# Five buffers instead of four for the convolution's constants and inverse transforms, and a new instruction order, in a memory-attention and S4-convolution kernel

## The chip, the cores and the metric

The kernel runs on one core of one Trainium2 chip. The metric is the device time of one execution in microseconds; the kernel before is given as the median of its runs. The profile comes from one further execution, taken by the hardware profiler, whose own time is told apart below.

## The reference

Two branches work on the same input of 2048 tokens and 512 channels, and a gate per token mixes them. Branch a is attention with a compressive memory: 32 heads of 16 channels, 4 segments of 512 tokens, each segment attending to itself by softmax and to the earlier ones through a running state. Branch b is a state-space (S4) convolution, 2048 long, per channel; the reference does it by FFT.

```
def _A_ref(x, wq, wk, wv, wo, beta):
    ...                                          # q, k, v: (B, H=32, N=4, L=512, Dh=16)
    for s in range(N):
        logits = einsum('bhqd,bhkd->bhqk', qs, ks) * scale + mask
        p = softmax(logits);  a_dot = einsum('bhqk,bhkd->bhqd', p, vs)
        num = einsum('bhld,bhde->bhle', phi(qs), M)
        den = einsum('bhld,bhd->bhl', phi(qs), z)[..., None] + 1e-06
        outs.append(g * (num / den) + (1.0 - g) * a_dot)
        M = M + einsum('bhld,bhle->bhde', phi(ks), vs);  z = z + phi(ks).sum(l)
    return o @ wo
def _B_ref(u, A_re, A_im, B_re, B_im, C_re, C_im, log_dt, Dskip):
    P = exp(dt*A * l);  K = einsum('dn,dnl,dn->dl', Cc, P, dt*Bc).real
    y = irfft2(rfft2(pad(u)) * rfft2(pad(K)))[:L] + u * Dskip
    return y
x = A_x
g = sigmoid((x * gate_w).sum(-1, keepdims=True))
return g * _A_ref(x, ...) + (1 - g) * _B_ref(x, ...)
```

## The kernel before

The kernel is written as a graph. Python code (`build_graph`) makes 1799 operations, each with the tiles that it reads and writes: loads and copies by DMA, matrix products on PE (TensorE), evictions from PSUM on ScalarE (ACT) or VectorE (DVE), exponentials on ScalarE, products on VectorE. A long string, `ORDER`, then fixes the program: it lists the numbers of the operations in one global sequence, with a letter for the engine where an eviction may go to either (a is ScalarE, v or none VectorE) and with the number of the buffer that each new tile takes from its pool. `Sched.replay` walks the string and appends each operation to its engine's program; `Sched.emit` places the semaphore waits. Every engine works off its program in order. SyncE (SP) issues 254 DMAs, in the order of the string too, so a DMA whose data or buffer isn't ready holds up those behind it.

The work that the text speaks of, by the names used in it:

- The head (0 to about 40 us): parameters are loaded, powers of the state matrix are squared up step by step (ScalarE squares at line 857, casts at line 865; VectorE at lines 858, 859, 866, 869), copied across partitions by DMA, and multiplied into tables (VectorE, lines 1353 to 1365).
- The attention, by segment s and group of eight heads: scores on PE, exponentials on ScalarE (lines 1197 and 1244, 128x2048 each), products with v, normalization on VectorE (1158 to 1161), and a transposing DMA (line 1309) that turns the result for the final product.
- The lagged rows (lag0 to lag3): short matmuls that make the convolution's kernel for one quarter of the lags each; three evictions on ScalarE, then four DMA copies into the tile KTT. The Fourier matrices multiply KTT, so the first of them, K0, waits for the last copy of lag3.
- The convolution (`conv`), 32 tiles u of frequencies. For each: a load CD(u) of 128x896 constants (229,376 bytes: 640 columns for the kernel's transform, 256 for the inverse), the transform K(u) on PE, an addition on VectorE (1492), the product Y(u) with the transformed input (1496), the inverse transform V(u) on PE, its eviction, and a DMA that scatters it into the tile V2. The CD buffer comes free when V(u) is done on PE. The pools in question are CD (4 buffers of 1792 bytes a partition) and V (4 of 1024).
- The tail: the final products with the output weights, the last transforms of V2, the mix and the stores.

Evictions all go through one function, so they stand at line 229 (ScalarE) or 230 (VectorE), plain DMAs at line 225, and nearly all matmuls at line 711. The loop body around the change:

```
CD = Tile(CDP, BF16)
S.dma(lambda CD=CD: ap(CD, n=896), lambda u=u: hC[u], 229376, w=[CD], key=kx - 6)
V = Tile(VP, BF16)
...
op("PE", c_pe("F", 512, 512), fi, r=[CD, Y], w=[PI], acq=[V])
S.evac(lambda V=V: ap(V, n=512), lambda PI=PI: ap(PI, n=512), 512, r=[PI], pw=[V])
```

Of the kernel before, what the change touches and what calls it, by code (L numbers as in the profile page):

```python
# [382 lines left out]
15/0 216/0 17/0 9/5 16/0 39/7/0 40 10/1 0/0 33/2/0 34a 204/0 11/0 28/0 30/0 12/3 31/4 32a 42/3 49/0 43/10 50/5 67/0  # L383
41/1 44/9 45 48/2 46 24/0 200/0 201 18/2 27/0 35/0/1 14/2 13/3 1237/1 47 55/5 414/1 57/11 51/12 56/7 7/0 58/4 36a 25/0
19 202 52 203/0 53 60/5 59 72/1 68/6 70/1 71a/0 69v 54 61/0 62/13 20 21 187/7 74/2 23/0 37/4/2 207/7 73 84/2 211/3/3/2
75v/5 267/5/1/0 3/0 1/0 87v/9 63/6 1248/0/0 38a 86/3 85 76 77 1250/6 842/0 65/0 182/1 208/0 64 1245/1/1 98/5 96/2 97
212a 229/7/0/0 268a 185/1 88 107v/1 183/0 186/0 1243/4 1249a 223/3 104/3 1246a 190/2 1251a 99a/6 217/0 66 230 106/3
108 105 224a 272/5/1/1 213 209/0 1252 1253/1/0 184 1244v 80/4 218a 273 118/1 116/3 1255/3 214/4/0 215a 1037v/0 191
119v/3 221/6 274 78/1 117 231 222a 843/0 1254a 257/0/0 258 128/2 131v/0 219/1 1256a 275 188/0 130/3 89 1038v 210/0 129
109 79 259 1041v/0 140/3 312/3/0/1 220a 142/2 1039v 844 627/0 628/0 234/0/1 132 143a/2 235 236 1040v 232 1045 92/6 120  # L390
1042 22 141 270/1/1 152/2 400/0 239/0/2 240 269 271a 189 1043/0 154/0 133 1046 121 1247 1238/1/1 144 1257 313a 1258/0
1044 1050 233/2/0 276 226 227 241 153 243/0/3 1239a 244 145 164/1 155a/4 1047 167v/7 225 1240/3 401/1 1241a 228
358/3/2 629 1266/0/0 1051 1048/0 1052 277/0 156 237/2 238 168 245 251/0/1 169 1053 252 402 1049 242 246 166/2 247
1264/1 359a 90/0 417/3 165 1267a 253 254/0 1054 1057/0 1056 288/0/3 248/0 314 176a/8 249 1265a 289 177 1242 255 157
418a 315/1/0 256 250/0 1271/2/1 290 1055 178 284/0/1 316a 91 1268 1058 1279/1 100/3 1272a 260 285 1261/3/0 1062 1259/2
1059 1269/1 1060/0 286 102/0 1061 1270a 279/0/2 280 4/0 1273 1262a 281 1260a 1274/3/1 261 262/4 355/1/3/2 1276/2
302/0/0 303 356a 282/1 283 287 1263 1275a 6/0 1067/0 263 1063 317/3/0/1 264 1287/0/0 1277a 304 318 101 1064 1066 319
360/2/1/0 1278 361 1068 320 291 292 1069 363 296/0/2 1288a 297 1295/3/1 321/0 362 2/0 1297/2 364 1070/0 110/0 293/5
1065 1071 298 331/0/3 332 365 1296a 1300/0 294 112/5 111 1298a 1299 295/1 205 1072/3/0 1073 1074 1080/2 124/2 1076/0
1077 1081 1078 333 1075a 1089v/0 299/1 1090v 300 322/0/2 1079a 1088v 1029/1 1091v/0 206 1095 403 1282/3/1 122/3 123  # L400
1087a 1093/0 278 1092 1280/0 29/0 323 1283a 324 1096 357 1094 473/3/1 301 305 1100 306 307/5 81v/5 339/0/1 340 136/7
1098/0 1101 1082a 325/2 134/0 326 1281a 406/0/2/0 341 308 125v/6 1097 1102 309 474a 407a 408 1099 345/0/0 1284 346
342/3 1103 347 1308/0/1 366 137a/9 343 421/1 1309a 327/0/2 328 422a 329 113a/3 1107/0 265 1285/0 1286a 1289 135
427/1/0/1 1104 376/0/1 330 310 377 1106 428 429 378 114 1105 409/0/0 410a 334 335 1085/0 148/1 336/1 344 348 146/2
367/0/2 368 138 1301/1/0 369 349 337 1108 350/0 419/0 126 1112 338/0 420a 372/0/3 373 1302a 1110/0 370/0 1303/1 371
1109 103a/1 374 93a/0 139 470/2/1/1 1304a 1113 1111 384/0/2 385 115 430 1305 1116 351 94 147 471a 352 478/1/1/0 95
# [12 lines left out]
1176/4 1177 1178 1179a 500 465 1323/3/0 1324a 501 466 1343 516/0/4/0 517 528/1 559/0/2 560 561 530/0 518 529 519 576
467 567/1/2/1 1180/0 1181 1182a 1191a/0 568 534 1189v/0 1190a 1187a 569 1347/1 536/0/1 537 538 535/0 1188v 585 570  # L420
1334/0 1195 1193/0 1185 1196 1184 586 587 1183 1200 1192 556/2 557 468 1201 699/3/0/0 1348a 700 1414/3 545/0/0 546
644/0 701 547 5/0 1202 539/1 1194 540 1327/3 846 645a 1328a 541/0/3 542 742/0/1/2 543 743a 1203 638/1 266/0 311 1197
1325/4 745/3/0 1374/0 1204 594/0/1 595 1339/0/2 1370/1 746a 596 1340a 544 548 549 1198/0 606/0/0 607 1350/3/6 608 1356
1335/0 1329/2 1336a 1332 469/0 354 1186 558 562 1354 589/0/3 590 1205 550/4 744 591 551 1199 552/0 642/1 581/1 643a
609/0 610 1212 563 611 598/0/2 599 1398/1 1206 1355 564/3 1326/3/1 1402/4 1330 1207/0 1410/2 1213 1344 1395/1 592/1
1448/0 593 597 565 1208 1331 600 566 612/0/0 1214 613 614 633/3/0/1 634a 571 572 1399/2/5 635 601 1403 615 602 664/0/3
665 1404 1210/0 1386/1 1209 616 617/4 861/3/1 862a 857/2 1211 603/1 858a 1216 655/0/1 656 694/3/2 1411/2/0 1217/0 1333
604 618 695a 1218 619/0 650/0/1/1 651 605 1220/0 1219 863/1 864a 676/0/2 1215 1221 677 652 1415 1230/3/0 1231 1232a
520 1226/1 1227 1228 659/0/0 1229a 698/0 693 1416 399 1378/4 1030/0 660 588 653 1031/0 702 657 484 632/1 1345 1407/0
678 666 521 1222/3 1223 1224 1225a 639 580 1477/0 1365/2 1484/1 1491/2 661 856 859/2 860a 658/0 672/0/1 1233 1236 1235  # L430
# [110 lines left out]
def build_graph(nc, es, A_x, A_wq, A_wk, A_wv, A_wo, A_beta, B_A_re, B_A_im, B_B_re, B_B_im,  # L541
# [1126 lines left out]
```

## Time and profile before

| | us |
|---|---|
| runs of the kernel before: lowest, median, highest of 3 | 283.33, 283.72, 285.1 |
| the profiled execution: its time | 286.65 |
| the profiled execution: its span | 284.9 |
| mean granted TensorE clock in it | 0.993 |
| busy: PE, VectorE, ScalarE | 252.6, 261.2, 253.6 |

The span runs from the first to the last instruction that the profiler saw on the core; the time of the execution contains what lies around it, 1.8 us here. The page gives busy time by engine, the span in 40 slices, the chain of work that ended last (followed back from the end: at each step to what released it, or to the instruction before it on its engine), groups of instructions, and DMA issues. The views used besides are a table of the span by stages, the waits, and the time line of one engine in a window, where neighbouring instructions of one kind are put together with their count. In that view a number in brackets is the time that the engine stood idle before the row, with what released it. PEld is the loading of weights into PE, which overlaps its matmuls; SPq is SyncE's queue of DMA issues.

### The profile page before, as it was taken

What the parts mean: (1) busy time and instruction counts of PE and PEld (TensorE: products, weight loads), DVE (VectorE), ACT (ScalarE), POOL (GpSimd) and SP (SyncE); (2) the same over time, 40 slices, a digit from 0 to 9 for tenths busy, and PEclk for the clock granted to TensorE, in tenths of its full rate; (3) what the DMA queues carried; (4) which work ended last, traced back from release to release, by engine and by line L of the source; (5) the groups of instructions that cost most, each with busy time, mean ns of one, the idle gap of its engine ahead of it and who ended that gap; (6) DMA issues with size and microseconds to landing.
All of it is one profiled execution on the core that took longest, in us unless ns stands there. A gap on an engine that the chain in (4) does not pass through costs nothing.

```text
span 284.9 us, 9231 instructions
## 1 busy us (share of the span) xinstructions
PE 252.6 (89%) x3871; PEld 158.2 (56%) x3921; DVE 261.2 (92%) x616; ACT 253.6 (89%) x315; POOL 5.0 (2%) x10
## 2 busy tenths in 40 slices
PE   4969788788888889889999989799999999999996
PEld 1624454465556556575675657565565555555653
DVE  2997999999999999999999989989999999998474
ACT  5998999999999999899879999989999999987312
POOL 5000000000000000000000000000000000000000
PEclk9997999999999999999999999999999999999999
DMA  5999646422213354417665587877588877693217
GB/s 121 258 234 177 169 104 168 129 65 59 63 58 85 81 153 127 144 34 116 164 194 147 150 205 204 216 209 213 162 211 212 245 215 225 155 166 91 74 39 258
DMA packets 59756, 43.44 MB, mean 152 GB/s; under 512 B 36162, under 2 KB 53699, under 8 KB 59715
## 3 DMA queue, kind: packets, MB, share of 16 engines
q1 hardware_dynamic: 59714, 42.85, 57.9%
q8 instruction: 31, 0.51, 0.8%
q14 instruction: 11, 0.08, 0.1%
HBM read 21.04 MB, written 7.86 MB: 101 GB/s over the span
## 4 chain that ended last, share of the span: by engine, by line
PE 40%; DVE 24%; ACT 21%; DMA 7%; issue 5%; SPq 2%; ACTq 0%; DVEq 0%
PE psum L711 38%; ACT sb L1244 7%; DVE sb L1353 6%; ACT sb L229 6%; ACT sb L1197 5%; DVE sb L1362 5%; DVE sb L1356 4%; DMA sb<-sb 3%; DMA sb<-c_DN 2%; DVE sb L1365 2%; SPq L225 2%; DMA sb<-in_B_B_im_dram 1%; DVE sb L1161 1%; ACT sb L857 1%; ACT sb L1028 1%
## 5 line engine op out<-in xcount | busy, mean ns | idle before, releaser
L711 PE MATMUL psum<-sb 128*128 128x17 bf16 (+17 forms) x3783 | 246.7, 228 | 26.4 <-ACT sb L229 6.6
L711 PEld LDWEIGHTS psum<-sb 128*128 128x128 bf16 (+6 forms) x3833 | 152.0, 101 | 116.8 <-issue 21.1
L229 ACT ACTIVATE sb<-psum 128x512 bf16<-128x512 f32 (+4 forms) x144 | 84.5, 634 | 7.5 <-PE psum L711 5.2
L1244 ACT ACTIVATE sb<-psum 128x2048 bf16<-128x2048 f32 x40 | 75.6, 1890 | 3.5 <-PE psum L711 2.9
L1197 ACT ACTIVATE sb<-psum 128x2048 bf16<-128x2048 f32 (+1 forms) x40 | 70.1, 1752 | 2.8 <-PE psum L711 2.8
L1353 DVE TENSOR_TENSOR sb<-sb 128x4096 bf16<-128x4096 bf16 (+3 forms) x24 | 37.5, 1563 | 0.7 <-DMA sb<-sb 0.7
L1362 DVE TENSOR_TENSOR sb<-sb 128x512 bf16<-128x512 bf16 (+1 forms) x48 | 24.6, 528 | 0.0
L1256 DVE TENSOR_TENSOR sb<-sb 128x1024 bf16<-128x1024 bf16 (+1 forms) x40 | 22.7, 575 | 0.0
L1496 DVE TENSOR_TENSOR sb<-sb 128x1024 bf16<-128x1024 bf16 x32 | 21.6, 684 | 0.3
L1356 DVE TENSOR_TENSOR sb<-sb 128x2048 bf16<-128x2048 bf16 (+3 forms) x24 | 20.4, 850 | 0.0
L1492 DVE TENSOR_TENSOR sb<-psum,sb 128x256 bf16<-128x256 f32 (+1 forms) x32 | 17.6, 553 | 1.9 <-PE psum L711 1.7
L232 ACT ACTIVATE sb<-psum,sb 128x512 f32<-128x512 f32 (+2 forms) x10 | 6.5, 664 | 12.7 <-PE psum L711 12.7
L230 DVE CAST sb<-psum 128x512 bf16<-128x512 f32 x22 | 15.0, 684 | 2.2 <-PE psum L711 2.2
L1161 DVE TENSOR_TENSOR sb<-psum,sb 128x256 bf16<-128x256 f32 x32 | 13.1, 411 | 0.2
L1365 DVE TENSOR_TENSOR sb<-sb 128x512 bf16<-128x512 bf16 (+1 forms) x24 | 12.6, 527 | 0.0
L857 ACT ACTIVATE sb<-sb 128x512 f32<-128x512 f32 x18 | 12.0, 667 | 0.0
L1158 DVE RECIPROCAL sb<-psum 128x16 f32<-128x16 f32 x32 | 8.0, 250 | 2.6 <-PE psum L711 2.6
L858 DVE TENSOR_TENSOR sb<-sb 128x256 f32<-128x256 f32 x18 | 7.4, 416 | 1.4 <-ACT sb L857 1.3
L1298 DVE TENSOR_TENSOR sb<-psum,sb 128x512 bf16<-128x512 f32 x12 | 8.2, 685 | 0.2
L1028 ACT ACTIVATE sb<-psum 128x512 bf16<-128x512 bf16 x12 | 7.4, 631 | 0.7 <-PE psum L1025 0.7
L865 ACT ACTIVATE sb<-sb 128x512 bf16<-128x512 f32 x11 | 7.8, 709 | 0.0
L1079 ACT ACTIVATE sb<-sb 128x512 bf16<-128x512 bf16 x12 | 7.8, 646 | 0.0
(79 smaller groups left out, 127.4 us busy)
## 6 DMA issues: line engine op xcount, KB each, us to landing
sb<-sb SPq DMA_DIRECT2D x64, 128.0 KB, 3.3
sb<-c_DN SPq DMA_DIRECT2D x32, 224.0 KB, 3.4
scr_Z<-sb SPq DMA_DIRECT2D x16, 256.0 KB, 2.4
sb<-scr_Z SPq DMA_DIRECT2D x16, 256.0 KB, 3.4
sb<-in_A_x_dram SPq DMA_DIRECT2D x5, 512.0 KB, 4.6
sb<-c_DN SPq DMA_DIRECT2D x16, 160.0 KB, 3.3
out_dram<-sb SPq DMA_DIRECT2D x7, 256.0 KB, 2.2
scr_O<-sb SPq DMA_DIRECT2D x12, 128.0 KB, 3.2
```

The costliest lines, as they stand in the source:

```text
L229: fa = lambda e: e.activation(dst(), src(), ACT.Copy)
L711: mm = lambda e, o_, l, r_, st, sp, **kw: e.matmul(o_, lhsT=l, rhs=r_, start=st, stop=sp, skip_group_check=True, **kw)
L1161: op("DVE", ("V1", 256), lambda e: e.tensor_tensor(ap(o1, gi * 16, [[128, 4], [32, 4], [1, 16]]), ap(T, dims=[[68, 4], [17, 4], [1, 16]]), ...
L1197: o = op("ACT", ("Ax", 4 * n), lambda e: e.activation(ap(pT, dims=[[512, 4], [1, n]]), ap(P, dims=[[512, 4], [1, n]]), ACT.Exp, scale=0.25 ...
L1244: o = op("ACT", ("Ax", 2048), lambda e, P=P, pT=pT: e.activation(ap(pT, n=2048), ap(P, n=2048), ACT.Exp, scale=0.25), r=[P], w=[pT])
L1256: op("DVE", ("V2", 128 * nb), lambda e, pT=pT, dims=dims: e.tensor_tensor(ap(pT, dims=dims + [[1, 128]]), ap(pT, dims=dims + [[1, 128]]), ...
L1353: op("DVE", ("V2n1" if n == 1 else "V2", 512 * n), lambda e: e.tensor_tensor(ap(tile, 2 * dst, [[2 * (sp - dst), 2], [2 * ne, 128], [1, 2 ...
L1356: op("DVE", ("V2n1" if n == 1 else "V2", 256 * n), lambda e: e.tensor_tensor(D_(), D_(), ap(tile, 2 * sp + ne * 128, [[-ne * 128, 2], [2 * ...
L1362: op("DVE", ("V2x" if sstep > 2 else "V2", 256 * n), lambda e, half=half: e.tensor_tensor(run(t2, n, 0, 1) if half else run(tile, ne, dst, ...
L1365: op("DVE", ("V2", 256 * n), lambda e: e.tensor_tensor(D_(), D_(), ap(t2, n * 128, [[-n * 128, 2], [2 * n, 64], [1, 2 * n]]), ALU.add), r= ...
L1492: op("DVE", ("V1", 512 - 32 * c0), lambda e, K3=K3, PK=PK, c0=c0: e.tensor_tensor(ap(K3, 32 * c0, n=512 - 32 * c0), ap(PK, n=512 - 32 * c0 ...
L1496: op("DVE", ("V2", 1024), lambda e, Y=Y, XAB=XAB, K3=K3, Ke=Ke, xo=xo, u=u: e.tensor_tensor(ap(Y, dims=[[512, 2], [1, 512]]), ap(XAB, xo, ...
```

## The change

Two pools get a fifth buffer each: CD, for the transform constants, and V, for the evicted inverse transforms. The V pool thereby overlaps in memory with one more pool of the earlier stage, whose last readers are the lagged matmuls. The rest is a wholly new `ORDER`: the same 1799 operations in another sequence, with other buffer numbers. The counts of instructions on each engine stay as they are; of the evictions that may go to either engine, ten move to VectorE and ten to ScalarE. A line of the string is shown for its form.

```diff
 ORDER = """
-15/0 216/0 17/0 9/5 16/0 39/7/0 40 10/1 0/0 33/2/0 34a 204/0 11/0 28/0 30/0 12/3 31/4 32a 42/3 49/0 43/10 50/5 67/0
...
+16/0 9/0 15/0 216/0 30/0 17/0 39/3/0 10/3 0/0 33/6/1 40 34a 414/1 31/0 204/0 28/0 11/2 32a 49/3 12/1 42/7 67/1 41/0
...
     V2aP = mkpool("V2a", 16384, 1, 2)
-    CDP = mkpool("CD", 1792, 4, 2)
+    CDP = mkpool("CD", 1792, 5, 2)
     XsPs.append(mkpool("Xsb", 4096, 3, 2))
     K3P = mkpool("K3", 1024, 4, 2)
     YP = mkpool("Y", 2048, 4, 2)
-    VP = mkpool("V", 1024, 4, 2)
+    VP = mkpool("V", 1024, 5, 2)
```

**SyncE at the start of the convolution**, before. The rows of shape 128x1x160 are the four copies of lag3; 128x896 are loads of CD (the two in a row behind 128x640, a load of another constant, are CD1 and CD2; the one behind the copies is CD3); the transposing DMA belongs to the attention.

```order
L225 DMA sb<-c_DN 128x896
L225 DMA sb<-c_DN 128x640
L225 DMA sb<-c_DN 128x896 x2
L225 DMA sb<-sb 128x1x160 x4
L225 DMA sb<-c_DN 128x896
L225 DMA sb<-scr_Z 128x1024
L225 DMA sb<-sb 64x1024
L225 DMA scr_O<-sb 128x4x128
L225 DMA sb<-c_DN 128x640
L1309 DMA_TRANSPOSE sb<-scr_O 128x1x512
```

The same place now: CD1, two copies, CD0 and CD3, the third copy, the transpose, the fourth copy.

```order
L225 DMA sb<-c_DN 128x896
L225 DMA sb<-sb 128x1x160 x2
L225 DMA sb<-c_DN 128x896 x2
L225 DMA sb<-sb 128x1x160
L1309 DMA_TRANSPOSE sb<-scr_O 128x1x512
L225 DMA sb<-sb 128x1x160
L225 DMA sb<-scr_Z 128x1024
L225 DMA sb<-c_DN 128x896 x2
```

The four copies stood together; now two loads of CD stand between the second and the third, and the transpose between the third and the last.

**ScalarE at the same place**, before. 128x40x12 and 128x40x8 are the three evictions of lag3, 128x2048 are exponentials.

```order
L1244 ACTIVATE sb<-psum 128x2048
L229 ACTIVATE sb<-psum 128x40x8
L229 ACTIVATE sb<-psum 128x40x12
L1244 ACTIVATE sb<-psum 128x2048
L229 ACTIVATE sb<-psum 128x40x12
L229 ACTIVATE sb<-psum 128x32x16
L1244 ACTIVATE sb<-psum 128x2048
```

And now:

```order
L1244 ACTIVATE sb<-psum 128x2048
L229 ACTIVATE sb<-psum 128x40x12 x2
L229 ACTIVATE sb<-psum 128x40x8
L1244 ACTIVATE sb<-psum 128x2048
L229 ACTIVATE sb<-psum 128x32x16
L1244 ACTIVATE sb<-psum 128x2048
```

The third eviction moved ahead of the exponential.

A little later on SyncE, CD10, CD7 and CD6 stand in this order (before: CD7, CD10, then the load Zx4 of transformed input, then CD6; now: CD10, CD7, the store of V0, CD6, and Zx4 seven places behind CD6). With five buffers CD6 takes the one that V3's matmuls free; before, it took the one that V4's freed. On PE, K6 stands at the same place of its program, with V5 now directly ahead of it instead of X15 (one matmul).

In the head, the parameter C_re goes to another buffer and is loaded ahead of C_im; of the powers, one square on ScalarE moves ahead of two evictions, and the cast of the seventh power behind an exponential, a square, an eviction and another cast.

**PE at the end of the program**, before. The run of 30 wide matmuls (128x512) holds five of K31, the last score block of four, and 21 behind it; 128x17 are products of exponentials with v.

```order
L711 MATMUL psum<-sb 128x512 x30
L711 MATMUL psum<-sb 128x17 x8
L711 MATMUL psum<-sb 128x512 x2
L711 MATMUL psum<-sb 128x17 x32
L711 MATMUL psum<-sb 128x512 x7
L711 MATMUL psum<-sb 128x128 x8
L711 MATMUL psum<-sb 128x512 x59
L711 MATMUL psum<-sb 128x256 x12
```

And now, where the first two rows are the last score block:

```order
L711 MATMUL psum<-sb 128x384 x4
L711 MATMUL psum<-sb 128x128 x4
L711 MATMUL psum<-sb 128x512 x3
L711 MATMUL psum<-sb 128x17 x24
L711 MATMUL psum<-sb 128x512 x12
L711 MATMUL psum<-sb 128x17 x16
L711 MATMUL psum<-sb 128x512 x6
L711 MATMUL psum<-sb 128x128 x8
L711 MATMUL psum<-sb 128x512 x57
L711 MATMUL psum<-sb 128x256 x12
```

Behind the last score block stood 21 + 2 + 7 + 59 = 89 wide matmuls, and now stand 3 + 12 + 6 + 57 = 78. The load of the output weights moved back in SyncE's program, to its 244th place of 254.

More of the change, by code (lines that the diff above doesn't have):

```diff
@@ L468 @@
[L468 to L470 removed]
+16/0 9/0 15/0 216/0 30/0 17/0 39/3/0 10/3 0/0 33/6/1 40 34a 414/1 31/0 204/0 28/0 11/2 32a 49/3 12/1 42/7 67/1 41/0
+44/1 13/4 14/5 24/0 48/4 45 27/0 50/2 18/1 19 20 200/0 201 46 1237/0 43/13 55/0 51/8 47 57/10 56/5 52 202 7/0 53 25/0
@@ new lines @@
+58/6 203/0 54 35/6/2 36a 60/2 68/2 59 72/1 69v/0 74/1 70/5 71a 73 84/2 182/0 21 62/0 1/0 187/3 37/7/1 38a 85/4 87v/9
+3/0 207/3 86 211/4/0/2 63/3 75v/6 267/0/1/0 88 99a/0 23/0 96/2 1243/6/0 268a 188/3 208/0 76 1248/3/1 1250/2 98/5 97
+842/0 272/5/0/1 185/1 89 212a 104/0 1251a 1245/7 61/9 190/2 107v/1 1244v 229/0/1/0 64/0 209/0 230 1249a 66 213 191/0
+77 106/7 1246a 189 108 105 210/0 116/2 186 183/3 1252 273 1255/2/1 109 117/6 118 217/4 1247 221/6 218a 222a 128/0
+119v/3 274 1253/3 65 130/1 184 275 223/7 214/4/0 224a 215a 78/3 231 120 131v/5 1256a 257/0/0 258 80/7 79 259 22
@@ new lines @@
+289 359a 254/1 255 290 1055 256 260 100/0 315/2/0 418a 316a 4/0 1268 248/1 1057/0 284/0/2 249 285 286 1056 250/0 1058
+1062 1269/3 1270a 1261/0/0 178 1060/0 404/0 1059 1273 279/0/1 280 1259/2 1063 1274/3/1 261 1262a 281 1260a 355/0/3/2
+262/4 1061 263 356a 101 1067/0 1066 314 1276/2 264 302/0/0 303 1064 282/0 283 287 1263 1287/1/0 1275a 1277a 317/3/1/1
+360/2/0/0 291 292 1278 304 296/0/1 297 1068 318 320 1288a 319 1070/0 293/3 361 362 294 1069 1297/1/1 363 1295/3 298
+321/2 364 1071 331/0/3 1296a 299/3 332 1298a 1299 1065 1080/1/0 6/0 300 8/0 295/1 1076/0 1077 1081 205 365 110/2
@@ new lines @@
+335 419/3 1109 350/2 1301/2 420a 1111 125v/3 82 83 430 336/5 1116 1117/0 1112 372/0/1 1302a 373 370/3 337 371 1083
+405/1 95 470/2/1/1 351 2/0 103a/4 374 138 384/0/3 146/3 385 1084 471a 386 1118 352/1 148/4 375 379 139 1305 1306/1
+1307a 478/2/1/1 479 380 338 114 390/0/2 391 415/0 392 147 1119 387/1 388 389 126 1113 408 1120/0 353 480 1313/2/0 1085
+432/0/0 433 1114 1121 393 394 416a 646/0/0 423 481 1115 366 1314a 434 395/5 381/3 441/0/1 396 442 425 149v/9 1310
+1122/2/0 1123 115 647a 382 1126/0 1124 158/0 1127 397/1 1128 383 443 5/0 159/7 431/1/1 1125a 192/5 160 170/2 1130/3
@@ new lines @@
+1157/0 1154 692a 1158 1155 162 163 494/0/1 495 1341/0 1160/0 446/1 526/1/0 531/0/1/1 460/2 447 1159 461 448/1 488/3
+496 489 493 502/0/0 1161 503 412 497 1166 1167/0 462 1338/2/1 1168 532 527a 1162 533 1342 265 504 508/0/2 509 475/1
+505/1 574/0/0/1 498 510 506 575a 553/0/0 554 1163 555 1169 1164 1170/0 1165 1349/3 1321/0 507 636/0/1 1370/2 511 512
+1346/2 637a 513/3 1351/5/1 1352a 1334/0 1398/1 1171 499/5 463/3/0/0 528/0 464 582/4/0/0 583 1322/1 514 845 1172/0/0
+1176/5 1173 1174 1175a 1177 1178 500 465 1179a 530/0 476 501/0 515 1323/3/0 516/0/2/1 584 579/1 466 517 1343 1324a
@@ new lines @@
+1206 563 564/2 610 1208 611 591 598/0/2 599 643a 1326/0/5 1213 565 1330 592/2 593 1331 597 600 566 1214 1402/4 571
+612/0/3 613 633/0/2/1 1344 614 1356 1399/3/0 634a 635 1403 601 1404 639 1209 615 616 664/0/0 1332 1374/3 311 602
+861/0/1 1210/0 665 617/3 862a 572 857/3 858a 469/0 655/0/2 656 694/0/2 695a 1414/1 1211 603/0 1216 618 1217/0 619/1
+650/3/1/0 1218 651 1386/4 1407/0 1184 744 1220/0 863/1 864a 676/0/1 1411/0/2 1415 677 1219 1215 1221 1226/1/0 652 1345
+520 1222/3 1223 1224 1225a 604 1416 693 1227 1228 1229a 1365/1 653 521 1230/0 580 1231 484 1232a 659/0/3 1484/3 660
@@ new lines @@
+1490/0 1419/0 1500 1494/3 1362/3/3 1390/0 1368 1501/0 752 1513/1/1 716 1369 1495/0/3 1496a 712 713 714 723/0/1 1514
+729 1506/1/0 1515/3 1388/0/2 1366 717 718 1507 724 1547/0 1367 1502/1/1 1526/3 1389a 735/3/4/1 1384/4 1483 1503a
+1519/1 1385a 1497 856 1408/5/0 1508/2 1509/3/2 1409a 736 725 737 719/0 738 720 802 722/0 726 730 1510a 1511 1394
+806/0/1 721/1 705 731 796/1 732/3 1032 684/1/1/0 797 1393 1387/1/7 807 1391 733 810/0/3 685 753 847/1 734 1527/0/3 686
+1392 1548/1/0 747/0 1561/4 687 1516/2/0 739 740 1520/3/2 808 1371/2 1528 811 1423/4/2 1517a 1424a 1412/5 1413a 1549
@@ new lines @@
+962 967/1 959 1003/0/0 1669/1 1661 963 1657a 970 971 964/5 965 966/0 975 976 977/4 978 979 941/0 1687/2 1473/3/2 1474v
+1004 841 942a 1471/2 1472a 994/0/3 984/1 985a 1469 1658 1670/0/3 1671a 1023/1/0/1 1651 1707/1 1708 1005 1476 1662/2
+1727/0 1728 1729a/0 1024 1025 1026 1709v/0 1688/2/3 1676/3 1689 1733/0 1695/3/0 995 996 998/0/2 1475 1696 1697/0
+1677/2/0 997/1 1734 1637 1678v 1735v/1 1701/3 1680/1 1702 1698/2/2 1679 999 1000 626 1699a 1690/1 1011/0/1 1012
+1681/0/0 1682 1663/2/4 1001 1002 1672 1006 1013 1007/0 1683/3 1008 1009/1 1015/0/3 1740/0 1703v/1 1664a 1010/2 1014
@@ L471 @@
+1783 1785v 1786a 1787
 """
```

137 lines of the change are left out of this document (50 added, 87 removed).

## The prediction

> **What bounds the kernel now.** I read the busy line of the page first, then the span cut into stages, then the chain that ended last, and at the places it names the time line of each engine.
>
> ```profile
> PE 252.6 (89%) x3871; PEld 158.2 (56%) x3921; DVE 261.2 (92%) x616; ACT 253.6 (89%) x315; POOL 5.0 (2%) x10
> ```
>
> Three engines are within four per cent of one another, so the page's shares name no bound. The stages do; the columns are the length and the busy time of PE, PEld, DVE, ACT and POOL, then clock, DMA share and GB/s.
>
> ```profile
> 0.00:27.00 27.00, 19.75 (x136) 10.39 (x139) 19.75 (x61) 22.04 (x42) 3.73 (x8) 0.94 0.95 207
> 27.00:120.00 93.00, 78.87 (x1563) 50.72 (x1578) 92.05 (x211) 91.90 (x122) 0.65 (x1) 1.00 0.40 108
> 120.00:165.00 45.00, 41.84 (x867) 29.38 (x878) 44.79 (x109) 41.88 (x51) 0.67 (x1) 1.00 0.53 130
> 165.00:190.00 25.00, 22.20 (x293) 15.21 (x293) 22.86 (x60) 22.68 (x25) 0.00 (x0) 1.00 0.81 213
> 190.00:262.00 72.00, 70.08 (x888) 40.07 (x899) 68.51 (x160) 68.96 (x69) 0.00 (x0) 1.00 0.73 194
> 262.00:282.60 20.60, 19.89 (x137) 12.45 (x138) 13.23 (x22) 6.15 (x10) 0.00 (x0) 1.00 0.31 109
> ```
>
> The head waits for transfers. From 27 to 165 VectorE is idle for 0.95 + 0.21 = 1.2 us of 138, so nothing but work taken off it helps there. From 165 to 282.6 PE is busy for 112.2 of 117.6 us: 2.80 + 1.92 + 0.71 = **5.4 us** of idle time are all that an order can win there. The largest pieces of it stand in the chain of the convolution's start (start, length, what):
>
> ```profile
> 161.67 3.98 DMA sb<-sb
> ...
> 165.74 1.74 PE psum L711 x18
> ...
> 178.02 0.62 PE psum L711 x3
> 178.64 6.35 DMA sb<-c_DN
> ...
> 185.04 5.21 PE psum L711 x53
> ```
>
> Two transfers end waits: the last copy of the lagged kernel rows, for which K0 waits at 165.74, and the constants of K6 (CD6), issued at 178.64 when V4's matmuls have released a buffer. The time lines give what the engines lost there (in brackets the idle time before, and its releaser).
>
> ```profile
> 165.74 1.74 PE L711 MATMUL psum<-sb 128*128 128x256 bf16 x18 [0.52 <-DMA sb<-sb]
> ...
> 185.04 5.21 PE L711 MATMUL psum<-sb 128*128 128x256 bf16 x53 [1.36 <-DMA sb<-c_DN]
> 186.45 1.57 ACT L229 ACTIVATE sb<-psum 128x512 bf16<-128x512 f32 x3 [1.57 <-PE psum L711]
> 185.80 0.42 DVE L1492 TENSOR_TENSOR sb<-psum,sb 128x256 bf16<-128x256 f32 x1 [0.27 <-PE psum L711]
> 188.52 0.69 DVE L230 CAST sb<-psum 128x512 bf16<-128x512 f32 x1 [1.10 <-PE psum L711]
> ```
>
> At K6 all three stop for about the same time: PE 1.36, ScalarE 1.57, VectorE 0.27 + 1.10 = 1.37. That is a stall with nothing beside it, and worth its length.
>
> **The buffers and K6.** A load of c_DN usually takes half of what CD6 took (least, median, most):
>
> ```profile
> DMA to landing us min/median/max: 2.3/3.4/6.4
> ```
>
> SyncE's issues around it:
>
> ```profile
> 175.12 2.62 SPq L225 DMA_DIRECT2D sb<-c_DN  x2
> 178.21 0.32 SPq L225 DMA_DIRECT2D sb<-scr_Z  x1
> 178.64 0.36 SPq L225 DMA_DIRECT2D sb<-c_DN  x1
> ```
>
> The two ahead are CD7 and CD10; CD10, freed by V3, is the second of the first row, whose bar ends at 175.12 + 2.62 = 177.74. With five buffers CD6 takes what V3 frees, one convolution tile earlier, and Zx4, a transfer of 256 KB, comes behind it. An issue takes 0.32 us, so CD6 goes out at about 177.74 - 0.32 = 177.42, 1.22 us earlier, and at the same 6.35 us lands at 183.77. PE came free for K6 at 185.04 - 1.36 = 183.68. What is left of the wait is 0.09, and V5's two matmuls now stand ahead of K6. **I take -1.3 us**; bounds 0 (it lands no earlier, because it is the queue that is slow) and -1.57, ScalarE's gap. On average the 32 loads get about 3 us more between release and use, but this is the only load that this trace shows PE waiting for:
>
> ```profile
> PE psum L711 <- DMA sb<-c_DN: 1.4, 1, 1.4
> ```
>
> So the other 31 loads' lead is priced at nothing, and so is the fifth buffer of the V tiles: no eviction of an inverse transform waited for its slot here.
>
> [...]
>
> **The lagged rows and K0.**
>
> ```profile
> 157.20 1.99 ACT L1244 ACTIVATE sb<-psum 128x2048 bf16<-128x2048 f32 x1
> 158.96 1.19 ACT L229 ACTIVATE sb<-psum 128x480 bf16<-128x480 f32 x2
> 159.78 3.63 SPq L225 DMA_DIRECT2D sb<-sb  x4
> 163.45 0.59 SPq L225 DMA_DIRECT2D sb<-c_DN  x1
> ...
> 166.42 1.29 SPq L1309 DMA_TRANSPOSE sb<-scr_O  x1
> ```
>
> Before, two of the three evictions of the lagged rows stand ahead of the 1.99-us exponential on ScalarE and the third behind it, and the four copies go out back to back from 159.78. After, all three evictions stand ahead of the exponential, but between the copies stand two loads of CD and a DMA transpose: 0.32 + 0.59 + 1.29 = 2.2 us of issuing, by the last two of these rows and, for CD0, the 0.32 us that an issue took at 178.21. How much earlier can the third eviction be? PE's run with its matmuls, and the loads that wait for the same matmuls:
>
> ```profile
> 156.68 1.27 PE L711 MATMUL psum<-sb 16*128 16x384 bf16 x56 [0.29 <-ACT sb L1244]
> 157.98 1.75 SPq L225 DMA_DIRECT2D sb<-c_DN  x4
> ```
>
> The run ends at 156.68 + 1.27 = 157.95, so the eviction can come forward from 158.96 by 1.0 us. If a copy lands as long after its issue as now, K0 comes 2.2 - 1.0 = 1.2 us later. Two smaller things work the other way: one of the four loads that went out ahead of the copies comes behind them (1.75/4 = 0.4), and PE has one short block less ahead of the lagged matmuls (0.2, an estimate from the length of such a block in its order). **I take 1.2 - 0.6 = +0.6**; bounds -0.5 (PE's wait of 0.52 goes) and +2.2 (nothing comes earlier). Behind K0 in PE's order stand K1, score blocks and the whole convolution, so a delay there is passed on; VectorE is idle for only 2.1 us from 165 to 190 and ScalarE for 2.3, and half of that already belongs to K6.
>
> **The head.** The load of C_re loses a wait on SyncE's queue, since it no longer reuses a buffer that PE reads. Two waits of VectorE are touched by the new order:
>
> ```profile
> SPq L225 <- PE psum L796: 2.0, 1, 2.0
> 26.83 0.76 DVE L858 TENSOR_TENSOR sb<-sb 128x256 f32<-128x256 f32 x2 [1.35 <-ACT sb L857]
> 39.46 2.29 DVE L1353 TENSOR_TENSOR sb<-sb 128x4096 bf16<-128x4096 bf16 x1 [0.67 <-DMA sb<-sb]
> 33.57 5.80 DMA sb<-sb
> ```
>
> The 1.35 us for a square on ScalarE should go, because that square stands earlier there. The 0.67 us for a copy of a power (the last row, issued at 33.57) should grow: its cast on ScalarE stands behind an exponential now and three smaller operations,
>
> ```profile
> 30.43 1.91 ACT L1197 ACTIVATE sb<-psum 128x2048 bf16<-128x2048 f32 x1
> 32.19 0.67 ACT L857 ACTIVATE sb<-sb 128x512 f32<-128x512 f32 x1
> 35.56 0.71 ACT L865 ACTIVATE sb<-sb 128x512 bf16<-128x512 f32 x1
> ```
>
> which moves its end by some 3.3 us to 33.9 and its issue from 33.57 to 34.2 at the earliest: 0.6 late. VectorE and ScalarE share the work of the next stage, so what one of them alone wins or loses counts half: -1.35/2 + 0.6/2 = **-0.4**; bounds -1.35 and +0.7 (the second wait doubles and the first stays).
>
> **The tail.** After the last score block 78 wide matmuls and 12 of half width are left, instead of 89 and 12. Their price is the pitch near the end, where 49 wide and 12 half ones ran:
>
> ```profile
> 270.00:281.80 11.80, 11.75 (x61) 1.00 0.33 122
> ```
>
> 11.75/(49 + 6) = 0.214 us, so 11 x 0.214 = 2.4 us of PE work move ahead of the last exponentials. PE is busy there too (70.08 of 72 us from 190 on), so moving work out of the tail shortens nothing unless it fills idle time. The load of the output weights is issued later, near 244 of 254, with about 1 to 2 us to spare. **I take 0**; bounds -1.9 (all of PE's idle time of 190 to 262 is filled) and +0.5 (a weight late by that much).
>
> Ten evictions go to VectorE and ten to ScalarE:
>
> ```profile
> L229 ACT ACTIVATE sb<-psum 128x512 bf16<-128x512 f32 (+4 forms) x144 | 84.5, 634 | 7.5 <-PE psum L711 5.2
> L230 DVE CAST sb<-psum 128x512 bf16<-128x512 f32 x22 | 15.0, 684 | 2.2 <-PE psum L711 2.2
> ```
>
> At 634 and 684 ns a pair costs neither engine more than 0.05 us each way, and the counts of instructions stay: nothing, with bounds of 0.5 either way.
>
> **Sum.** -1.3 + 0.6 - 0.4 + 0 = -1.1 us. The profiled execution took 286.65 us, 1.8 more than its span of 284.9, and its sum is 285.55. The median of the runs is 283.72, or 0.9898 of the profiled one, and 285.55 x 0.9898 = **282.6 us**.
>
> **Rivals.** (a) The waits only change places and the time stays, 283.7. For it: from 165 on three engines are near their limit, and a released stall of 1.3 meets the +0.6 and whatever comes late next, such as Zx4, now behind CD6. Against it: at K6 all three engines stood still. (b) The longer lead also removes the short waits of PE that the chain doesn't name: half of 5.4 us, and 0.7 of the head, 3.4 together: 283.25 on the profiled scale, **280.4**. Against it: most of these waits are for ScalarE and not for loads. (c) Slower: the last lagged copy goes out behind the DMA transpose, K0 is 2.2 us late, every slot of the convolution is released so much later, and CD6's gain is lost with them: 286.65 + 2.2 = 288.85, **285.9**. It decides whether the third eviction leaves ScalarE more than about 1.6 us earlier than 159.7; if not, this holds. (d) The fifth buffer is there but the loads go out as before, since SyncE issues in order and is held by something else ahead of them; only +0.6 - 0.4 remain: 286.85, **283.9**.
>
> **How the numbers follow.** Forecast 0.46 (own range 281.3 to 283.6), (a) 0.18, (b) 0.18, (c) 0.12, (d) 0.06. The bounds of the terms add up to -5.8 and +3.9; not all fall on one side. The range reaches to (b) and nearly to (c): 280.0 to 285.6. A difference under about 1% (2.8 us) is what a measurement of this kernel can't tell from none. Faster by more means under 280.9: most of (b) and an edge of the forecast, 0.20. Slower by more means over 286.6: an edge of (c), and something late that I don't see, 0.09. Within 1%: 0.71.
>
> **What would show it.** In the profile after: CD6 issued near 177.4, relative to K0, and PE's wait for c_DN gone (first term); PE's idle time before K0 at about 1.1 us, still ended by a copy (second); VectorE's 1.35-us wait gone and that at L1353 at 1 us or more (third); from the last score block to the end the span shorter by about 2.4 us, with PE's idle time from 190 on unchanged near 2.6 (fourth). A new wait for a DMA of over 2 us anywhere behind 165 would make the prediction wrong upwards; PE's idle time behind 165 under 3 us, downwards.

## The result, and the profile after

The kernel with the change took 283.25 us (median of 20 runs, 282.55 to 284.47). The kernel before, run beside it, took 285.51 us (20 runs, 282.78 to 291.21). The ratio is 0.9946 with a 95% interval of 0.9923 to 0.9968: half a per cent faster, within the range of the forecast and under the one per cent that the prediction called no change. (The ratio leaves out executions that lie over 1.5% above the fastest of their kernel, so it is nearer to one than the two medians.) The lowest times of the two kernels, 282.78 and 282.55, are almost the same. What differs is the spread, and that turned out to be the subject of this case.

The page of the profiled execution (283.67 us, span 281.9), busy line and granted clock:

```profile
PE 256.6 (91%) x3921; PEld 156.5 (56%) x3921; DVE 260.0 (92%) x616; ACT 254.5 (90%) x315; POOL 5.0 (2%) x10
PEclk9999999999999999999999999999999999999999
```

And the clock row of the page of before:

```profile
PEclk9997999999999999999999999999999999999999
```

The fourth slice of before, 21 to 28 us, has a 7: for a part of it PE's granted clock was lower. The prediction read the row of stages with its 0.94 for the head and passed over it. The same stages after the change:

```profile
0.00:27.00 27.00, 18.65 (x146) 9.24 (x150) 21.64 (x70) 23.60 (x43) 3.69 (x8) 1.00 0.83 192
27.00:120.00 93.00, 82.00 (x1651) 51.76 (x1653) 92.14 (x211) 92.19 (x125) 0.65 (x1) 1.00 0.46 122
120.00:165.00 45.00, 42.47 (x821) 28.21 (x816) 43.79 (x103) 41.43 (x46) 0.66 (x1) 1.00 0.49 122
165.00:190.00 25.00, 24.68 (x322) 16.40 (x320) 24.79 (x64) 23.92 (x27) 0.00 (x0) 1.00 0.77 217
190.00:262.00 72.00, 71.82 (x897) 40.54 (x896) 68.18 (x157) 66.52 (x66) 0.00 (x0) 1.00 0.72 188
```

From 165 to 262 PE is busy for 96.50 of 97 us. The first place where the two executions part is the head. PE's time line there, before and then with the change:

```profile
18.48 0.38 PE L711 MATMUL psum<-sb 128*128 128x512 bf16 x1
21.35 4.18 PE L711 MATMUL psum<-sb 128*128 128x512 bf16 x25 [2.49 <-ACT sb L229]
```

```profile
17.25 2.12 PE L711 MATMUL psum<-sb 128*128 128x512 bf16 x9
20.04 0.39 PE L711 MATMUL psum<-sb 128*128 128x512 bf16 x1 [0.68 <-ACT sb L229]
20.62 1.04 PE L711 MATMUL psum<-sb 128*128 128x512 bf16 x4 [0.19 <-ACT sb L229]
22.11 1.04 PE L711 MATMUL psum<-sb 128*128 128x512 bf16 x4 [0.46 <-ACT sb L229]
```

Before, PE has a pause of 2.49 us; with the change it is cut up into 0.68, 0.19 and 0.46. The windows of before that follow the pause (length, PE's busy time, granted clock, DMA share, GB/s) show what comes of it:

```profile
21.00:22.00 1.00, 0.65 (x2) 0.74 1.17 339
22.00:23.00 1.00, 1.00 (x4) 0.50 1.00 136
23.00:24.00 1.00, 1.00 (x4) 0.50 1.09 234
24.00:25.00 1.00, 1.00 (x4) 0.55 1.10 249
25.00:26.00 1.00, 0.69 (x24) 1.00 1.29 116
```

PE works at a granted clock of 0.50 from 21.49 to 24.90, 3.41 us, and so does 1.7 us less, an estimate (half of 3.41). The clock's next change in this profile is at 284.32, behind PE's last matmul: 259.42 us later, which is 76 times 3.413. The exponentials of this execution start 1.5 us later than the same ones with the change around 45 us, and 1.9 us later at 146.

The second place is the start of the convolution. The issues and PE with the change:

```profile
175.97 0.32 SPq L225 DMA_DIRECT2D sb<-c_DN  x1
164.11 1.74 PE L711 MATMUL psum<-sb 128*128 128x256 bf16 x18 [0.76 <-DMA sb<-sb]
180.57 9.68 PE L711 MATMUL psum<-sb 16*128 16x384 bf16 x111 [0.17 <-ACT sb L1244]
DMA to landing us min/median/max: 2.3/3.4/5.4
```

The first row is CD6, issued 11.9 us behind K0's start instead of 12.9; the last is for all loads of c_DN. K6 lies within the last PE row, which has no pause, so its wait is gone. K0's wait for the last lagged copy has grown from 0.52 to 0.76.

### The profile page after: what moved, and what is told of

The parts are those of the page before. It is cut to its first block, busy times and chain, and to the rows that moved or that the text cites. A ratio compares the mean times of both kernels' runs of the same rounds, so it can differ in the third digit from the quotient of the medians.

```text
span 281.9 us, 9260 instructions
## 1 busy us (share of the span) xinstructions
PE 256.6 (91%) x3921; PEld 156.5 (56%) x3921; DVE 260.0 (92%) x616; ACT 254.5 (90%) x315; POOL 5.0 (2%) x10
## 4 chain that ended last, share of the span: by engine, by line
PE 41%; DVE 29%; ACT 14%; DMA 6%; SPq 5%; issue 3%; ACTq 0%
PE psum L711 41%; DVE sb L1353 8%; DVE sb L1362 5%; ACT sb L1244 5%; DVE sb L1356 5%; SPq L225 4%; ACT sb L229 4%; ACT sb L1197 3%; DVE sb L1365 2%; DMA sb<-sb 2%; DMA sb<-c_W 2%; DMA sb<-in_A_x_dram 2%; DVE sb L1161 1%; DVE sb L858 1%; DVE sb L859 1%
## 5 line engine op out<-in xcount | busy, mean ns | idle before, releaser
L711 PE MATMUL psum<-sb 128*128 128x17 bf16 (+20 forms) x3833 | 252.2, 229 | 21.4 <-ACT sb L1197 5.8
L711 PEld LDWEIGHTS psum<-sb 128*128 128x128 bf16 (+7 forms) x3833 | 151.1, 101 | 119.0 <-issue 17.7
L229 ACT ACTIVATE sb<-psum 128x512 bf16<-128x512 f32 (+5 forms) x145 | 84.7, 631 | 4.6 <-PE psum L711 3.4
L1353 DVE TENSOR_TENSOR sb<-sb 128x4096 bf16<-128x4096 bf16 (+3 forms) x24 | 37.6, 1566 | 0.0
L232 ACT ACTIVATE sb<-psum,sb 128x512 bf16<-128x512 f32 (+2 forms) x10 | 6.4, 666 | 10.8 <-PE psum L711 10.8
L230 DVE CAST sb<-psum 128x512 bf16<-128x512 f32 x21 | 14.2, 685 | 1.0 <-PE psum L711 1.0
L857 ACT ACTIVATE sb<-sb 128x512 f32<-128x512 f32 x18 | 11.9, 667 | 0.0
L1572 DVE SCALAR_TENSOR_TENSOR sb<-psum,sb 128x512 bf16<-128x512 f32 x8 | 5.7, 747 | 4.1 <-PE psum L711 3.9
```

What stands on the lines that cost most here:

```text
L229: fa = lambda e: e.activation(dst(), src(), ACT.Copy)
L711: mm = lambda e, o_, l, r_, st, sp, **kw: e.matmul(o_, lhsT=l, rhs=r_, start=st, stop=sp, skip_group_check=True, **kw)
L1353: op("DVE", ("V2n1" if n == 1 else "V2", 512 * n), lambda e: e.tensor_tensor(ap(tile, 2 * dst, [[2 * (sp - dst), 2], [2 * ne, 128], [1, 2 ...
```

## The experiments

Every run also records its mean granted clock. A fall to one half for 3.41 us of 284 makes 0.994; two make 0.988 (of the 99 executions of before 28 lie at 0.993 or 0.994 and 13 at 0.988). With these numbers the executions fall into two groups, and the table gives them for every kernel (before: the 99 executions beside the three sets of experiments; the change: 20 and 12). Below, a fall is a stretch at half the clock, and "at full clock" means executions without one (the profiled execution of new back, whose trace has no clock rows, counts as such).

| kernel | executions | clock under 0.998 | median of the others, us |
|---|---|---|---|
| before | 99 | 52 | 283.62 |
| the change | 32 | 0 | 283.26 |
| new head | 12 | 4 | 283.59 |
| old head | 12 | 7 | 283.54 |
| new front | 12 | 0 | 284.69 |
| new back | 12 | 5 | 285.34 |
| pause filled | 12 | 3 | 283.81 |
| both filled | 12 | 5 | 283.94 |
| five buffers only | 12 | 4 | 284.40 |
| CD6 earlier | 12 | 5 | 283.73 |
| copies together | 12 | 0 | 283.05 |
| pause made | 12 | 9 | 283.73 |
| new order, four buffers | 6 | 6 | none |

For the kernel before, the 47 executions at full clock have a mean of 283.76, the 28 with one fall 285.36, the 13 with two 286.06 and the 11 with more 288.50. All 99 have a mean of 285.04, the change's 32 of 283.44: 1.60 us less, of which 283.76 - 283.44 = 0.32 at full clock and the other 1.28 by the falls.

**Four crossings of the two orders.** The operations up to a cut in the one order, then the rest in the other; buffer numbers are given anew where the crossing needs it (12 to 46 operations).

```diff
-ORDER: before                     CD, V: 4
+new head:  change[:340]  + before without these, CD, V: 4
+old head:  before[:340]  + change without these, CD, V: 5
+new front: change[:1050] + before without these, CD, V: 4
+new back:  before[:1050] + change without these, CD, V: 5
```

> Four buffers; the order of the change for its first 340 operations (to about 55 us), then the order of before. Theory 1, two separate gains: the profiled executions were apart by 1.9 us at 45 us, because two waits of VectorE in the head went, so this kernel is about 1.5 to 1.9 us faster than before (ratio 0.994), and still waits for CD6 for about 1.3 us. Theory 2, clock: the head of the profiled execution of before ran at a granted clock of 0.94 and that of the change at 1.00, so the 1.9 us belong to that execution and not to the order; this kernel is as fast as before (ratio 1.000 within 0.002). Theory 3: a gain in the head is taken back in the stage from 27 to 120, where VectorE and ScalarE have no idle time and must do the same work; the ratio is 0.998 to 1.000 and the shift shrinks from 1.9 to under 0.5 us by 120.

New head: ratio 0.9993 (0.9955 to 1.003). At full clock it takes 283.59, before 283.49 in the same set: the new head in itself brings nothing, as theory 2 said, and in its profile K6 waits for CD6 again (us in all, number of waits, the longest):

```profile
PE psum L711 <- DMA sb<-c_DN: 1.0, 1, 1.0
```

> Five buffers; the order of before for its first 340 operations, then the order of the change. Theory 1: the gain behind 165 us alone, about 1.2 us (K6 no longer waits for CD6, K0 waits a little longer): ratio 0.996. Theory 2: the whole gain of the change, ratio 0.9946. Theory 3: as theory 2.

Old head: ratio 1.0008 (0.9967 to 1.005), 7 of 12 executions with a fall. At full clock 283.54. No theory expected this: with the old head the gain of the change is gone. The profiled execution shows its fall not in the head but behind the cut, for two lengths of 3.4 us; the windows around it:

```profile
52.00:55.00 3.00, 1.15 (x14) 1.00 0.10 5
55.00:58.00 3.00, 2.76 (x44) 0.66 0.31 96
58.00:61.00 3.00, 3.00 (x111) 0.50 0.71 191
61.00:64.00 3.00, 3.00 (x51) 0.70 0.03 8
64.00:67.00 3.00, 2.68 (x63) 1.00 0.06 21
```

Again a stretch in which PE does little, a thin one, stands just ahead of the fall. No single pause in it is long: PE waits 0.77 us, does two matmuls, and waits 1.32 us. The 3.42 us up to the fall, of which PE is busy for 1.36:

```profile
52.57:55.99 3.42, 1.36 (x15) 1.00 0.08 1
```

> Four buffers; the order of the change up to the start of the convolution (first 1050 operations, about 162 us, with the split copies of the lagged rows), then the order of before. Theory 1: 1.6 us faster than before at K0, as in the two profiles, and then the 1.4-us wait for CD6 again: ratio 0.994 to 0.995, the same as the kernel with the new head alone plus 0.3 us for the later copies. Theory 2: slower than before by 0.3 us, ratio 1.001, since the split copies cost and nothing else is gained.

New front: ratio 1.0022 (0.9992 to 1.0052). No fall in 12 executions, but 284.69 at full clock: the old back with renumbered buffers is slower here (PE waits for CD loads twice, 1.0 us together), so it tells nothing of the size of theory 1's gain. It does tell where the falls of before are decided: ahead of 162 us.

> Five buffers; the order of before for its first 1050 operations (to about 162 us, four copies of the lagged rows together), then the order of the change. Both theories: K6 doesn't wait, K0 waits 0.5 us as before, so 1.3 us faster than before, ratio 0.9955. If the gain behind 162 us needs the loads that the order of the change has already issued ahead of that point, the wait for CD6 stays at over 0.7 us and the ratio is 0.998.

New back: ratio 1.0058 (1.0026 to 1.0091), slower than either parent. K0 and K6 do as expected, but K13 waits 1.7 us for its load, as in no other profile with the change's five buffers; the buffers are renumbered here, and whether that is the reason wasn't tried. 5 of 12 executions show a fall. The four together: falls came only with an old piece ahead of 162 us (16 of 36 executions with one, 0 of 12 without, 0 of 32 with the change), and no crossing beats the kernels that it is made of.

**The pause, filled and made.** If the pause is the cause, filling it must take the falls away from before, and making one must bring them to the change.

```diff
+    def ff(e):                      # in its order directly ahead of the matmul that waits until 21.35
+        for _ in range(9):
+            i_ = mm(e, ap(Pf, n=512), ap(ident, n=128), ap(ident, dims=[[0, 4], [1, 128]]), True, True)
+        return i_
+    op("PE", c_pe("F", *[512] * 9), ff, r=[ident], w=[Pf])
```

> The kernel before with nine additional matmuls of 128x512 (their result is not used) put on PE into its pause of 2.49 us in the head, from 18.9 us; all else is as before. Theory clock: the pause is what makes the granted clock fall to one half for 3.4 us in about half of the executions (19 of 35), depending on how it falls into the fixed windows of 3.41 us; with the pause filled, no execution shows a clock under 0.998 and the median falls from 285.0 to 283.5 us, by 0.5 per cent, although PE has 1.9 us more to do. Rival: the clock falls for another reason (the stage from 27 to 120, heat, the run); then some half of the executions still show a clock of 0.994 or less and the median stays, or grows by up to 1.9 us.

Ratio 1.0008 (0.9969 to 1.0047), 3 of 12 executions with a fall, against 10 of 29 of before in the same set. The theory said none. It is no clear decrease either: with one in three for before, 3 of 12 is about as many. None of the three was a single fall (0.993 or 0.994), of which before has 28 in 99; two lay at 0.987 and one at 0.85, with 297.87 us.

The second attempt filled the thin place near 55 us too:

```diff
+    op("PE", c_pe("F", *[512] * 4), fg, r=[ident], w=[Pg])   # behind the first matmul of xl1.11
```

> The kernel before with both of its thin places on PE filled: nine additional matmuls of 128x512 in the pause at 18.9 us, and four behind the first of the two matmuls of xl1.11 near 55.6 us, where the kernel with the old head showed its fall of the clock (their results are not used). Theory clock: no execution under 0.998 (before: 10 of 29 on the last chip), median 283.5 to 283.9. Rival: the falls have another cause, and a quarter or more of the executions still show one.

Ratio 0.9981 (0.9945 to 1.0016), 5 of 12 with a fall, two of them single, against 23 of 35 of before in the same set: not what the theory said. The profiled execution was one at full clock, so it can't show where the others fell. Then the other way, on the change:

```diff
 PE, the order of the change:
-xl1.3a  tok0.0  tok0.2  xl1.3b  tok0.3
+xl1.3a  xl1.3b  tok0.0  tok0.2  tok0.3      (xl1.3b waits for ScalarE)
 ScalarE: the evictions of tok0.0 and tok0.2 behind those that stood ahead of xl1.3b
```

> The change with one matmul (the second of xl1.3, which waits for ScalarE until 20.0 us) moved ahead of the two token projections of 17.3 to 18.9 us on PE, and the evictions of these behind it; the work is the same. PE's two short pauses there (1.2 and 0.5 us) become one of about 2.7 us. Theory clock: about half of the executions show a clock of 0.994 or less (none of 20 with the change) and take 2 to 2.5 us longer than the others; the median rises from 283.3 to 284 or more. Rival: the pause itself costs nothing and the clock stays at 0.999 or more, as with the change.

9 of 12 executions show a fall, against none of 12 of the change on the same chip, and the median is 285.55 against 283.32. At full clock it takes 283.73 (three executions), so the moved work itself costs about 0.4 us and the fall 1.7 (one) to 2.3 (two). PE's time line and the windows of its profiled execution:

```profile
17.11 0.39 PE L711 MATMUL psum<-sb 128*128 128x512 bf16 x1 [0.61 <-ACT sb L229]
19.91 6.70 PE L711 MATMUL psum<-sb 128*128 128x512 bf16 x17 [2.41 <-ACT sb L229]
17.00:21.00 4.00, 1.48 (x4) 0.74 0.76 159
21.00:25.00 4.00, 4.00 (x10) 0.50 1.00 257
25.00:29.00 4.00, 3.31 (x24) 0.91 0.80 152
```

A pause of 2.41 us and then 17 matmuls in 6.70 us, at half the clock for two lengths (6.8 us, an estimate from the clocks of the three windows). That this pause makes the clock fall is shown; that it is the pause of before that does it there in all cases is not, since before still fell with it filled. The two distances between changes of the clock in the profile of before, 3.41 and 259.42 us, fit steps of 3.41 us, and the same program falls in one execution and not in the next (52 of 99 of before); that the place of a pause within such steps decides it was a theory and isn't shown. PE need not be idle all the time ahead of a fall. In the profiles at hand PE was busy for these shares of the 3.41 us ahead of a fall: 0.27 (before), 0.32 (five buffers only, below), 0.40 (old head) and 0.41 (pause made). Counted in steps of 3.41 us from the changes of the clock, the thinnest stretch between 10 us and the tail without a fall had 0.47 (new head).

> The change itself beside the three others, on the same chip. Theory clock: all executions at 0.998 or more, median 283.1 to 283.5. Rival: the missing falls belonged to the chip or the day of the first measurement, and some appear here.

283.32 us (12 runs), ratio 0.9955 (0.9931 to 0.998), no fall. The result holds in a second measurement.

**The buffers.** Five buffers in the order of before, only the numbers of the buffers differing:

```diff
-    CDP = mkpool("CD", 1792, 4, 2)
+    CDP = mkpool("CD", 1792, 5, 2)
-    VP = mkpool("V", 1024, 4, 2)
+    VP = mkpool("V", 1024, 5, 2)
```

> The order of before with five buffers for CD and for V; only the numbers of these buffers differ. Theory queue: CD6 still stands behind Zx4 on SyncE, which waits for X10 and X11 to 178.2, so it goes out no earlier, and K6 waits as before; in executions at full clock the time is that of before, 283.5 within 0.3. Rival: CD7 and CD10 go out earlier, the transfers of CD6 meet less traffic, it lands over 1 us earlier, and the time at full clock is 282.4 to 282.8. The granted clock falls as often as with before under both, since the head is the same.

Ratio 1.0026 (0.9993 to 1.0059), 284.40 at full clock: no gain, rather a loss. Its waits for loads and copies:

```profile
PEld psum L711 <- DMA sb<-c_DN: 1.7, 2, 1.1
PE psum L711 <- DMA sb<-sb: 1.5, 1, 1.5
```

K6 still waits (the longer of the two waits of PEld), and K0 now waits 1.5 us. No load goes out among the four copies that K0 needs; they even go out 0.4 us earlier than before (from 159.37 instead of 159.78). But the last one lands 4.9 us behind its issue instead of 4.0, while the load behind the copies goes out 1.5 us earlier (161.91 instead of 163.45), and from 162 to 164 us the transfers move 181 GB/s instead of 132. That the earlier loads slow the copies is likely and not shown. This profile also has a fall in the head, at 21.3 us behind a pause of PE of 2.70, the second one seen at this place in the order of before. So in this order a buffer alone gains nothing; and one step further, with CD6 pulled ahead:

```diff
 SyncE, the order of before, five buffers:
-CD7  CD10  Zx4  CD6
+CD7  CD10  CD6  Zx4
```

> The order of before with five buffers for CD and V and CD6's load directly behind CD10's on SyncE, ahead of Zx4. If K6's wait is worth its length (1.3 us) also in the order of before, it is gone and the time at full clock is 282.3 to 283.2, against 283.5; if the wait only moves, as with the five buffers alone (K0 1.6, K6 1.0, 284.4 at full clock), 284 or more. The clock falls as often as with before.

Ratio 0.9975 (0.9942 to 1.0009); at full clock 283.73, against 283.85 of before in this set. K6's wait is gone, and another has come up, at K18:

```profile
222.34 3.87 PE L711 MATMUL psum<-sb 128*128 128x512 bf16 x19 [0.95 <-DMA sb<-c_DN]
```

That looks like rival (a), the wait that changes its place. One profile doesn't show that the one wait came from the other: with the pause filled, where CD6 stands as before, K18 waited too, 0.44 us. The other way round, the order of the change without its fifth CD buffer:

```diff
-    CDP = mkpool("CD", 1792, 5, 2)
+    CDP = mkpool("CD", 1792, 4, 2)
 SyncE: 15 loads of CD move back behind the V(u) that frees a buffer
```

> The order of the change with four buffers for CD: 15 of the 32 loads of CD move back on SyncE to behind the inverse transform that frees a buffer; V keeps five. If the fifth buffer of CD is worth the wait at K6, the wait for CD6 is there again (about 1.3 us) and others of up to 0.5 us with it: 284.5 to 285 at full clock, against 283.25. If PE's order alone made the difference, 283.3. No execution shows a clock under 0.998, since the head is the change's.

299.80 us, ratio 1.0508 (1.0433 to 1.0583): 16 us slower than the change, ten times what was expected. PE waits for these loads 8.0 us, and for what hangs on them besides, in one place for 4.19 us:

```profile
PE psum L711 <- DMA sb<-c_DN: 8.0, 4, 3.3
222.62 10.15 PE L711 MATMUL psum<-sb 128*128 128x512 bf16 x116 [4.19 <-DVE sb L1496]
```

Those pauses also bring falls of the clock, in the profile at 223 and at 247 us, behind stretches of 3.41 us in which PE was busy for 0.16 and 0.24; all six executions have some, against the expectation. The order and the buffer belong together: the order of before lives well with four, that of the change doesn't, with the 15 loads placed as they were here.

**The lagged copies.**

```diff
 SyncE, the change:
-CD1  copy copy  CD0 CD3  copy  transpose  copy
+CD1  CD0  copy copy copy copy  CD3  transpose
```

> The change with SyncE's order mended at the start of the convolution: CD1, CD0, then the four copies of the lagged rows together, then CD3 and the transposing DMA. The last copy goes out at about 158.2 instead of 160.8. Theory: K0's wait of 0.76 us for that copy goes, PE is busy without a pause from there to the end, and so all of it comes through: 282.5 at full clock instead of 283.25. Rival: from 165 on PE is not what sets the end everywhere, or the transfers are slower than their issue, and less than 0.3 us comes through.

283.05 us (282.54 to 283.95), ratio 0.9963 (0.9937 to 0.9988), no fall. K0 waits for nothing, in the row of 158.05 here:

```profile
158.05 7.18 PE L711 MATMUL psum<-sb 32*128 32x512 bf16 x110 [0.46 <-ACT sb L1244]
```

But in the second profile of the change itself K0 doesn't wait either:

```profile
157.51 7.18 PE L711 MATMUL psum<-sb 32*128 32x512 bf16 x111 [0.46 <-ACT sb L1244]
```

So the 0.76 us belonged to one execution. Against the change's 283.25 and 283.32 the gain is 0.2 to 0.3 us between different sets, less than these runs can tell from none. It is faster than before; whether it is faster than the change is open.

## Why the prediction was right, and where it was not

The forecast was 282.6 from a sum of -1.1 us; the measured difference, by the ratio, is 0.54% of 285.5 or 1.5 us. The size was about right, and that is largely luck. The sum was one of waits and of shifted work, and in executions at full clock the whole change is worth 0.3 us over all sets, and 0.5 beside its second measurement. Most of the 1.5 us comes from falls of the clock, which the prediction doesn't have. The level was luck too: the three runs of before that it started from have a median of 283.72, near the 283.62 of executions at full clock, where the 20 runs beside the change have 285.51.

- **K6, -1.3.** The mechanism was right: CD6 goes out about 1 us earlier relative to K0, and in four profiles with the change's order throughout (or with one place moved) PE never waits for a CD load. Even more than was said: it landed after 3.1 us, not 6.35, and lay ready 3 us before K6. In the pair of profiles the wait was worth its length: the last exponential ahead of K6 starts 1.5 us earlier with the change (181.02, before 182.51), the next one 2.8 us (185.07, before 187.90). But the 1.36 us came from one execution; with four buffers and the old order behind 162 us, the waits of PE for CD were 1.4 (before), 1.0 (new head), 1.0 (new front), 0.7 (pause filled) and 0 (both filled), on average 0.8.
- **The lagged rows, +0.6.** A small size, wrong by the execution: 0.76 - 0.52 = 0.24 in the first profile, and no wait in the second.
- **The head, -0.4.** The step that failed. The 1.35 us of VectorE were put down to the order on ScalarE. In truth PE ran at half its clock for 3.4 us, ScalarE waited for PE, and VectorE for ScalarE. ScalarE's rows of before:

```profile
23.61 0.60 ACT L229 ACTIVATE sb<-psum 128x512 bf16<-128x512 f32 x1 [0.73 <-PE psum L711]
25.19 1.08 ACT L229 ACTIVATE sb<-psum 128x512 bf16<-128x512 f32 x2 [0.47 <-PE psum L711]
```

Where the head of before ran without a fall at this place, with the same order on ScalarE, VectorE doesn't wait there: in the profiles of old head, new back, pause filled, both filled and CD6 earlier (its row follows). With the fall of five buffers only it waits 1.13.

```profile
24.94 0.76 DVE L858 TENSOR_TENSOR sb<-sb 128x256 f32<-128x256 f32 x2
```

The order of the change cut PE's pause up, and none of its executions fell. All falls of before together are worth 1.28 us on average, and nothing in an execution at full clock; how much of that belongs to this one pause is open. The term's other half, a longer wait for the copy of a power at L1353, didn't come: with the change that row stands at 38.13 without a pause.

```profile
38.13 2.29 DVE L1353 TENSOR_TENSOR sb<-sb 128x4096 bf16<-128x4096 bf16 x1
```

- **The tail, 0.** From the end of the last exponential to the end of the last addition on VectorE it took 20.7 us before and takes 18.4 now, so the 2.4 us that were moved show. They were paid ahead of it: the exponential that starts at 245.51 before starts 2.7 us earlier with the change, at 242.79, but the last one ends only 0.7 earlier (261.8 before, 261.1 now).
- **The bound of 5.4 us** that PE could win behind 165 was too wide. The page of before has 3871 matmuls beside 3921 weight loads, so 50 records are missing, and their time was counted as idle. By the prediction's own rows 12 of them are behind 165 (888 beside 899, 137 beside 138); at 0.214 us for a wide one, that is up to 2.6 of the 5.4 us, an estimate. So the prediction's sign for a larger gain, less than 3 us of idle time behind 165, came up (0.5 us to 262 with the change, with all 3921 records) and meant little.
- **The rivals.** (a), waits that change places, is nearest to what the order of before does with a fifth buffer, by one profile of each kernel. (b) would have been 280.4. (c), the late copy, wasn't seen in the change. (d) has a time near the measured one, 283.9, but not its reason: CD6 did go out earlier.

**Left open**: with one thin place of before filled, 3 of 12 executions still showed a fall, and with both 5 of 12; no profile caught one. So there is at least one more place ahead of 162 us in the order of before where the clock falls in some executions; which, wasn't found. Where the 4 falls of new head come from isn't known either: its thinnest stretch, the one of 0.47, contains a wait of 1.78 us for a load, and a longer such wait is one candidate. What the fifth buffer of the V tiles does by itself wasn't run, nor what makes the 0.3 us at full clock.

## What to carry to other kernels

Read the row of the granted clock before the rows of waits: here a wait of VectorE of 1.35 us came from PE at 0.50 of its clock for 3.41 us, and not from the order on ScalarE. Add up PE's busy time over any 3.4 us of its time line, even where PE is not the bound there: here a fall came behind two pauses of 0.77 and 1.32 us as well as behind one of 2.41. And judge a small change by the executions at full clock and by the share of the others, apart. A buffer more pays only with an order that uses it, and a wait for a load in one profile is one draw: look at a second before pricing it in full.

## What was not expected of the hardware

- Pauses of PE go with falls of its clock: in every fall ahead of the tail that a profile of this case shows, PE had been busy for 0.16 to 0.41 of the 3.41 us in front of it (one pause of 2.41 to 4.19 us, or 0.77 and 1.32), and the clock was then 0.50, for 3.41 us in before and for about twice that in old head and pause made. That such a pause brings falls is shown once, by the made one: 9 of 12 executions against 0 of 12. One fall costs 285.36 - 283.76 = 1.6 us on average, and in the profile of before it lies in a stage where PE isn't even the busiest engine.
- Whether it happens differs by the execution: 52 of 99 for before. An estimate of the share, from PE's busy time in one profile of before: its time line from 10 us on is divided into stretches of 3.41 us, and for 0.57 of the places where the division can begin, one of them is busy for under 0.42 (the most ahead of a fall was 0.41). That it can begin anywhere no run shows. The same for the made pause gives 0.73, and 9 of 12 were measured; for the change 0, and 0 of 32. Elsewhere it doesn't fit: 0.63 for five buffers only, where 4 of 12 fell, 0.28 for old head (7 of 12), and 0 for new head, pause filled, both filled and CD6 earlier (4, 3, 5 and 5 of 12). One profile is one draw of the pauses too: in that of CD6 earlier, whose head is that of before, the pause is 1.75 us instead of 2.49.
